# Causal corners of the expert batches added by VectorE, fewer four-byte softmax chunks, and a new order table

## The chip, the cores and the metric

One NeuronCore of a Trainium2 chip runs the whole program. The metric is the device time of one execution in microseconds (us), and lower is better. The kernel before takes 612.18 us (median of three runs, 612.18 to 612.55).

## What is computed

A first attention has 8 heads in each of 4 batches over 768 positions, each query sees only the keys of its own hash bucket. Its output, 512 wide, feeds four causal attention "experts" per batch, which a top-2 gate mixes.

```python
mask = q_bucket[:, :, :, None] == k_bucket[:, :, None, :]
scores = np.where(mask, scale * np.matmul(q, k.transpose(0, 1, 3, 2)), -1e9)
attn = softmax(scores)
x = np.matmul(attn, v)            # (B, S, 512) once the heads stand side by side
logits = x @ w_gate               # the two best experts of each row, softmax weights w
for e in range(E):                # E = 4
    q, k, v = x @ wq[e], x @ wk[e], x @ wv[e]
    scores = np.where(causal, -1e9, scale * (q @ k.transpose(0, 2, 1)))
    ye = softmax(scores) @ v @ wo[e]
    out += (w of expert e, 0 where it isn't among the two) * ye
```

## The kernel before

The work is cut into units: 32 heads `("L", b, h)` and 16 experts `("M", b, e)`, which the list `seq` puts in a row: the eight heads of batch 0, then the heads of each later batch with the experts of the batch before it between them, and the experts of batch 3 at the end. A unit's place in the list is `pos`, from 0.

Each unit is an attention over 768 by 768 scores. `max_steps` forms the scores once on TensorE into the two PSUM buffers `mx`, and VectorE takes row maxima from them into `pm` (`pmw` for the first heads). `shift_steps` turns the maxima into a row of the query operand. `s_unit` forms the scores a second time, in chunks of up to 512 columns in the three PSUM buffers `st`, nine chunks for a head and six for an expert. For a chunk ScalarE takes two exponentials, `p` in four bytes and `ph` in two; GpSimd subtracts them into the remainder `pl`; and TensorE multiplies, for each block of 128 columns, `ph` by the upper half of v (`vh`, `mvh` for experts), `ph` by its lower half (`vl`, `mvl`) and `pl` by the upper half, all into the PSUM tile `o`, which `normalise` empties on VectorE into `xp` (heads) or `yn` (experts).

Two choices in `s_unit` concern us.

- Chunk 4 (`WHOLE`) of a head with `pos` under `NWHOLE` is kept whole: one exponential into a four-byte tile `pf`, no remainder, and per block one four-byte matmul by `vf`. With `NWHOLE = 12` these are the eight heads of batch 0 and the first four of batch 1.
- An expert's blocks on the diagonal need the causal corner. In batches that aren't in `MASKV`, TensorE adds it with one more 128x128 matmul of `mask_t` by the identity into the chunk, ahead of the chunk's second matmul. In batches in `MASKV`, here batch 3 alone, VectorE adds `mask_t` to the finished block in PSUM, and the chunk's exponentials wait for that.

`vproj_steps` makes v of the experts and the gate's logits, for each of six row tiles of a batch: TensorE into a PSUM buffer `misc`, ScalarE copies the upper half (`mvh`), VectorE forms the lower half (`mvl`), and ScalarE or VectorE copies four columns of logits (`lg`).

Around these run loads, halves and copies of operands between partitions (DMAs `qk<-qk`, `qk<-M`, all issued by SP's queue), transposes and projections. None of it is issued as written: a `Recorder` notes each operation, and `schedule` (all instructions are issued at line 183) puts them in the order of the table `ORDER`. For each step the table names the next operation, which engine takes it where there is a choice (`copy` may go to ScalarE or VectorE, some remainders to VectorE or GpSimd), and how many filler matmuls on the tile `busy` stand ahead of it. Each engine then works through its own part strictly in order. Line numbers of the profile are therefore all L183, and tile names tell the operations apart.

Of the kernel before, what the change touches and what calls it, by code (L numbers as in the profile page):

```python
# [211 lines left out]
MASKV = (3,)  # L212

ORDER = (
    "c-rlJX^bT2d0u^A-S^#9)z#Hqec#9QOwUZubkEGr%+9gPy}3M>BE4K*wnBljgy^6sSdb`LzLX$jC_r)|IdG6fN}@!8%mju5<X;5A2y6sF{v<G9|L_k(K%D%E6XpG?yLV=m%ZL=0<nFQ`"
    "u#fGj<E!_3-sgSZueymOS(bR7m!mVhfcQ902b^h9dwZSBE#Ig1smPWxIaNhLj1aY)&SbQXmN7F{W;O1!IP^u`u!}Y)m|K{toz_{l#fXTe1eYDMh{{)sMT(+UR#w&vYlV2Jc~J~<nS7<v"
    "Zu^B&{qLs2YPHsE)~k&|g$m-JU>6JdEFg#?KNAJbl2TeMd4+U3c<wp<#TRqUW;5Gpq&jSy)=TNaL(e@&IaS-f%9qsW+?A({OOFaya}PcG*rV3tfxef?2*QI8p2<G+P&(^l-@o|r!2jIm"
    "KIdy1<J+Eh{kr!FPgM<b>$e{N&EIVPhIy(pSm_|=@0sSH($EE5$*Da6vvVO5+5~j#IHJ~y)Y#liZ_LmfkEPKlyDLeh)fpm5l9sC8s{ib>jsEGUpZ28$obQX;!vrb7m8jDZJEG_*^+yyX"
    "tDGiKb|1Y3j%B%5r+DTTus3cv&h_i^=x||Om6bDRw3U^sM^GLVYa7Z^->m`EgR58Dt+6^9jrw-kto1t!J+r;64zx<S{Ip)x^+I8Jd08yWDonkiC~&cv9K2RDo)`5M1%e_9sl{`4A6c&X"
    "?;o*zfMd5gcLv#U3IIW~I5V0+&4}yk%Gz2wofZRARijAO6*aBKvIjHnjYc^^lDu#n1Ops8X^!)6i&CkSO2eT|&&fy;Yd>TA`tiS;+#(5S>U?Sf%L_wK3{$Bfv^1mtx^0@?1RDHRpA6R!"  # L220
    "4gDompWp@6!>+3KXRsMXYsx7@7HkLzBulT?*N?$<1zEBHl9}N5{!n&o!zh>Ka<eHn8k#07Y~?pMWicy5B(I5U!cfV%g#we$v+ZRDFXeKqTaTjZG*VIhw%}{usNLihS|JGY;ZppC#l=NK"
    "GoJq<lM37IOh{+bY1j2>2z0uY_8L(Tc<{EAo&iEwk^>{3&;MyEK6B=bcL>o4yvAZ<#agI)DW#H1nGh8Vn_24!xd|-QHDt@3hMQb}#VB_qLoXE@jfPb~mi4_>>whFEQqdanbo8ZKwpeVp"
    "yPaOIT!y!p@T1U}q3~l|Di%r!HcKb)ukyvXP+lmP%a0WPftD)>bvHgd%w{9ESj@PP<+)8MbU-vlqbQdP!U$w4=!lbR^(&QTbLju_gO$qVXP&8Cx?F}qV_bwo;+t%BN8~(KF##bB3!gdI"
    "29dznq<VTMn>#ob39==_bMbKuhx+PqWHTB1nw-w%C@G7@6ql~eu*Gd{!SToApN$i^?)n72KOFilWW!R<bG<+NGa^1-y3^_8^9wLp^?IsSLp3)jp8`-@1gX{H_yic$S{laZY#S0d<)_xx"
    "b}sMiEcRgsv^B$x8#mgoz8WiEF`FIJw!YY)zVHRjKJz(wd;3iDuyJuq*G(e<qhpQ09$<Cx+_@njfNOKTdUG*>Y)~z}LqN6Ls;a5=L4q4M1_QOUSTpLCFB+Yb5Ze<}I;~386YIiKP_0H~"
    "-U+F^4f9a3fi6YIyBV-b#w#PADWuXTB7XL)dnQ4ySq|JFlXp4CfjGg`x&9tH?Z%5I-~f5MIpla=t8xCkWz~Y<@Q^uh%yl#CSPsGBl5OoStgfEAIgO9Zu)2ETLU85EmGr_T!14o@buIzR"
    "S`Lz!)+x0^pE|X5@fcKPcjJKx)G@uaHQL)l5KI&fmsbxDS4SfO1aW(9irrmjxV{e4GrD~FvUAB>USD0il>7xD$aWJZbYo+Gd3kel8IcgPOPibQieW4n!vqKuMbKfh<tONC`<E^~x_|ND"
    "mmUKAi-#V%aPh(Y!*iFkCv^QkK*~;LRZ>-pQ0dI6GYXv7+Eq4;@pyYY-b=8xWtztLacXl4<AoJnKfitpHZ~6QeZyFP7J_x^`bdFGIDJ|hq3szKB*Hlr4)DMOr<GxEskjWI{m0we@O-nh"
    "DGLujy!NzmH9t^Fmr56{3m2NjbLWZ=Xv>o+F1+$efqD7mLZ|TA&#Ir%{<cv1^c26JAgkEacL{i^Fpj^i2EO}Efd9rDzW@5`-fOQdn0l(sjeh&L1)M5dFO^Dektm$wP?V9Vw&(FFN7pS&"
    "*CD8eE<c8AH9=AGc`i?ss^5>ROt(_0NY$!VrZOc4J~Z+N2M0j8e6!hV4mXEu!^a<gytzuQDBo!COAi9#D+x9)Z{m%OCpONVdyHEcJu+IjcI|6lLl3_C>Vy0H`w`pWb}q5{lD_!>rJo*;"  # L230
    "7e)zy374O}JOL!a=6K^#boMy@))CZ))_?ix)#snDoPGA$e*&lshZj$u-aGxB@6a^=yT40+`-N|Pi+ldlBrGqy@u|O0K)?R_a|bVNJWqY%8{hpdZ1@)7muUR)uVZ@ajW?LDzYd^Zd+oJf"
    "r<cz@y}bS~x5n?W+*iNKaliK}$8lR6H{N-X<39iS&r|p_470g8{u-dcz542_+*eq3_$77%*x>VzKF+etRdAlXFvT<64Tcd#K3XgZLKuE`gJt2bPx1URT>I{2o?luXz3{>dX6k{#*|R*~"
    "gTNnLU!$JlfXLUh#<VzHDRRG>)z};h>YF<}JnSBHx_dv{>hA9Dw!2ggxE%3g{usd3C@KM8t?pE-RRw0)j7xu7jC(^Q%c`tqR_gVPoG6GSud6*dSm8XeTJ2YVSnavlrE*yU(UK&ji-Jn3"
    "_lnNCOL02!4vxd~5E~AEEM*bCSzbCuw2OdYZq4;v$<hl9V=(bXVd^HrVi-zLo&gf586#l<Qj-{)KbeKfIsw5n1;fxZI$PvP+WwnK_GXz-lF|}U3d$P{{$Xk)ic8`IZBe`Qjjq@eMMaUM"
    "f|$eEEplM?<(FTEm}K~6{shRl1dVSz#Y^IEJpuUjDj)O0LO2;uCgTf^AUHf+aF(}Cr(?Q?X|P<i$1qT~iRP*FAG}G+H$e;kOq?N=qBZs}InKNZng(|KcZU5sE8YrL_>@3CWu*rs5jJIb"
    "{jtY(S&n;%Wf%7r$JSfHiCmTDnslS_e3(`OhWQiXz;QPL?o|DVwvPKOy4E692VxkVK87mHpNF-<U^EKD(VB*bpm@1#5YXwNF=}+DGTs>8g2O5BV!N%ovW$rwV!DG{VzXA)mY1to;2?6C"
    "1NxD=SOsQ-b2<GSj3r02n`k30fjd5u+|2p&S&$_TCFw+K48vfWHs~@>FBgkEm(QnCosP_L#9xVyoy(PTeBy?hCm<%yE0?P|6#7iP&Zdd|VG@gg=#9T2ElnoFt%qh;HkRc_JiQSvJRODx"
    "S1#+erAeA?+XnbT4HMcctn9E-rDCP(DcO{a5^HR3X2tPXgCg+en;;@vL1tqkpsBPkLFhK58M^gvsamTA@01B-U~W2{Oa4eX;AX`&X3G5$w5dF#>nEg!Qg5~dS&)9I)@WohkpMZqD~j8M"
    "B^P2>6c+=L;y9hN);WgV)LGrs8bfxKWmO)6%!^{7#<IdOWQ7BEAJWy}bRAMwkrjEOSdzpaF|Y;?o<|IO0u1v*h36U40SP>pVwjB$hSQkcT{te#6e49aCu!NVEFf?s<`_u*TfKhZcYzJ3"
    "7&hWVi4!fB<wAm)EeWC2XTmm=2%YU~3kwS-V!l~@<Bd1y)!vVOq?ZR|X8+|9z&>e$WRN(T7W@5Tvs#D3z|%}2U&$j<#7^2Yy40d3JfZ2j>*gwzFq>r@<_Nvsk9(rqVOoN!O<epodD?)M"  # L240
    "+NcPm%@E;4eZdpT9nfYeo0Z_b6$FIk$j{~ePY%j%c--sL6Aw<idd6`gHxoR)9_n^rr<zS{(XL$q$H>#*^Bj)$wNN2F8+38td;UvmTUl}y)`ae~fAOMh9LF}R>+vLwbv+vcC&M57;0I$o"
    "QrFjmtuVc@to|cabs=0mb%tXdUP(patLZHHl)?~m*LS5gN&3{MEI~xNAS^En9hhh7c1VR`CZ)QrO7Z{t(^gmM*p|$1@O2&v4s_b8b{w7t+_r7iBV9Km!$l~pE|{t$E{KArkxE5Ra|G0y"
    "rZYsHY3?LgUSxUB;cXjZc60OKz}RQ>(;SU?U>(%an+$9~gEs-j0wd%94Z2K=bY_d*B*!hj4K7?Dm6oGv-3FSd+rR{`&VXXNRijc_s!07Kln3R?zb)Gf3si3b>R6R#p&lf{TP}+frhw|*"
    "xX^CI<+xsd>fn|v__g{%BFGGcs!GzkungVY$D1^hr#&xMDxs)Q$YwAM0|f90`Fsy*tsp{W$|#1Qi=b3cH4zXDE;f%9qBP+oS|OK)Y9m3WtB}T(|3(G~8J={fa$f6bxYatyP9PAS8%1J9"
    "g`@f7a5R#<f@hkNtNu|6l8dyCUB+^xf^CcO%1Ukp>D(e=0T=@n<b;x>&!n&@s%=eFRj9toGk@hPK>|_sQ-y-(iNzF=>O5pi_Clhp5sW9D9&c@>>A-Q^sahRhg3vpYmsZ44YMzn;3d+)%"
    "tt~OTx3_)zG~OLY+rp_+g0Q(M814|m`~uUG+D?>-1JlEIB}kNFk}jG3eL<l2)c``0VUr~*XJtZXL(+R47MeJgXhci+F?)>bLL!iSI35gy)S^!@B)|+Fv23l@t8q}FnJIe}u`cGrn>$*T"
    "3y0qFJTLjDM@zJ#(LAUgVvnC7H+|(q@qgVEWGD?-fXRlbwM0l0dN6>h!y{>Jja}d{P=jN!@HQa2mq(<XL>w1IE{5}!4LNljOH;5e7J3eFmw`(!mo0d=!W5ZNt%e!C`YoZ?%T^#iYHhyS"
    "mgAdcw$wNdrcP7{)u?J|(v4%FGV%J|Zj{S;%>kirJ|D*Ib}^09<#M$eR4SPaaQFNSzjFS(3!516^1;DhEN`WP3GF?bw&+yy)-*Lu=hc>~W*5t9y0<|W3NN+W+^!a{@=!Y(2y9os&*I*M"
    "d_g@h(@~izdtPC)GQr*+!|av}Birw5T8<$JVDpes)~|tf_?Bb2nd$OLcZvg@=UaTUiT+rw*A=;{C&!UxGBf7J2Aw@zSdh#N%RUAK(X>8AqD$7qS~3_UzLDk9VtQr*A^%o5S4eC<HBCTX"
    "Q(3+At6EWw6Q#?rlWn2Q>-x?0f?8x`2#q;TbyfAt)Uv{|Wm$%)07dGQRT(I+DATSF(iddb&sw(Z$;kF>+X8X0H1o3rut`#vsx=spIeC}{EzZ_7l}D5t37;>UmmJ5ie`edBk-Bn_Qd01t"  # L250
    "W~quH$vs)S9nw_cKTREv1eREXJ{0O&Adkn^>C?ZWs%NnzOPd;eCd#6D4Nkly(hxSSg8O}%Ya~XxK|OdgJI;ax*&G|OnQohHwancyH6`63T&mZ#T5WNuR(m`N(az3}-qaET($i(3-E&)P"
# [1214 lines left out]
```

## Time and profile before

| | us |
|---|---|
| median of 3 runs | 612.18 |
| the profiled execution | 612.32 |
| its span, first to last instruction | 610.5 |
| TensorE busy | 591.4 (97%) |
| VectorE busy | 524.0 (86%) |
| ScalarE busy | 516.8 (85%) |
| GpSimd busy | 471.5 (77%) |

The granted TensorE clock is full throughout. Busy time of TensorE is no measure of its rate, because matmuls overlap: a 128x512 matmul in two bytes is shown 0.38 us long, while the next one starts 0.22 us after it. What a matmul costs is read from the distance between starts. 1.8 us of the execution lie outside the span.

### The profile page before, as it was taken

The page shows a single profiled execution, that of the slowest core. Times are in us where ns is not written, and L with a number is a line of the kernel's source. Part 1 is how long each engine was busy: PE and PEld are TensorE (multiplying, and loading weights), DVE is VectorE, ACT ScalarE, POOL GpSimd, SP SyncE. Part 2 cuts the span into 40 slices and gives each one's busy share as a digit, 9 for nine tenths or more (in the row PEclk, how much of TensorE's full clock was granted, in tenths as well). Part 3 has the DMA queues.
Part 4 walks back from the last instruction along what each step waited for, and adds up shares of the span by engine and source line. Part 5 has one row for each costly group of instructions (what it writes and reads, how often), then busy time and mean ns, then how long its engine had stood idle before and what let it go on. Part 6 is the DMA issues. An engine that isn't in the chain of part 4 may idle for free.

```text
span 610.5 us, 20339 instructions
## 1 busy us (share of the span) xinstructions
PE 591.4 (97%) x7754; PEld 432.8 (71%) x7754; DVE 524.0 (86%) x1440; ACT 516.8 (85%) x1132; POOL 471.5 (77%) x540
## 2 busy tenths in 40 slices
...
GB/s 188 169 189 195 81 146 68 56 99 48 153 40 58 41 87 61 102 104 32 92 89 87 37 119 101 58 83 73 68 87 75 45 48 42 16 21 28 87 79 104
DMA packets 36313, 51.22 MB, mean 84 GB/s; under 512 B 8212, under 2 KB 26104, under 8 KB 36216
## 3 DMA queue, kind: packets, MB, share of 16 engines
...
q8 instruction: 61, 1.00, 0.7%
q14 instruction: 36, 0.29, 0.2%
q10 hardware_dynamic: 160, 0.00, 0.0%
...
## 4 chain that ended last, share of the span: by engine, by line
PE 67%; DVE 17%; ACT 8%; issue 3%; POOL 2%; DMA 2%; SPq 1%; DVEq 0%; ACTq 0%; POOLq 0%
PE misc L183 22%; PE st L183 19%; PE o L183 16%; PE mx L183 10%; DVE pm L183 6%; ACT p L183 3%; ACT ph L183 3%; DVE qk L183 2%; DVE xt L183 1%; DVE misc L183 1%; POOL pl L183 1%; DVE pmw L183 1%; DMA natq<-in_q_dram 1%; SPq L183 1%; ACT xt L183 1%
## 5 line engine op out<-in xcount | busy, mean ns | idle before, releaser
L183 POOL TENSOR_TENSOR pl<-p,ph 128x512 f16<-128x512 f32 x370 | 409.4, 1126 | 111.3 <-ACT p L183 32.4
L183 PE MATMUL st<-qk 128*128 128x512 f16 (+12 forms) x928 | 229.7, 325 | 2.1 <-ACT p L183 1.0
L183 ACT ACTIVATE ph<-st 128x512 f16<-128x512 f32 x372 | 214.0, 609 | 15.2 <-PE st L183 11.1
L183 ACT ACTIVATE p<-st 128x512 f32<-128x512 f32 x372 | 215.9, 609 | 11.7 <-PE st L183 8.9
L183 PEld LDWEIGHTS <-ph 128*128 128x128 f16 x2880 | 168.1, 98 | 35.5 <-issue 6.5
L183 DVE TENSOR_REDUCE pm<-mx 128x2 f32<-128x512 f32 (+1 forms) x248 | 162.9, 673 | 11.2 <-PE mx L183 8.3
L183 PEld LDWEIGHTS <-pl 128*128 128x128 f16 x1440 | 133.3, 97 | 16.8 <-issue 4.1
L183 PEld LDWEIGHTS <-qk 128*128 128x128 f16 (+4 forms) x1248 | 109.1, 98 | 46.9 <-issue 9.2
L183 PE MATMUL mx<-qk 76*128 76x512 f16 (+2 forms) x464 | 134.3, 326 | 7.2 <-DVE qk L183 4.5
L183 PE MATMUL o<-vh,ph 128*128 128x65 f16 (+1 forms) x1104 | 138.8, 194 | 0.3 <-DVE xp L183 0.3
L183 PE MATMUL o<-vh,pl 128*128 128x65 f16 (+1 forms) x1104 | 138.8, 193 | 0.3 <-POOL pl L183 0.3
L183 PE MATMUL o<-vl,ph 128*128 128x64 f16 x1104 | 138.1, 192 | 0.0
L183 PE MATMUL misc<-xt,wqk_h 128*128 128x384 f16 x256 | 58.6, 325 | 0.0
L183 DVE CUSTOM_DVE_ANT_0 scrap<-mx,causal 128x512 bf16<-128x512 f32 (+2 forms) x96 | 44.4, 462 | 8.8 <-PE mx L183 7.0
L183 DVE TENSOR_REDUCE pmw<-mx 128x2 f32<-128x512 f32 x68 | 44.9, 681 | 2.3 <-PE mx L183 2.0
L183 PE MATMUL o<-mvh,pl 128*128 128x65 f16 x336 | 40.6, 193 | 0.6 <-DVE yn L183 0.6
L183 PE MATMUL o<-mvl,ph 128*128 128x64 f16 x336 | 40.9, 192 | 0.0
L183 PE MATMUL o<-mvh,ph 128*128 128x65 f16 x336 | 40.6, 193 | 0.1
L183 POOL TENSOR_TENSOR vl<-vf,vh 128x384 f16<-128x384 f32 x32 | 29.5, 928 | 11.1 <-PE misc L183 5.1
L183 PEld LDWEIGHTS <-xt 128*128 128x128 f16 x324 | 29.6, 97 | 10.7 <-issue 1.8
L183 PEld LDWEIGHTS <-wqk_h 128*128 128x128 f16 x256 | 24.0, 97 | 14.5 <-issue 1.6
L183 PE MATMUL misc<-wvg_h,xt 128*128 128x260 f16 x192 | 32.1, 274 | 0.7 <-ACT row L183 0.7
...
## 6 DMA issues: line engine op xcount, KB each, us to landing
qk<-qk SPq DMA_DIRECT2D x128, 96.0 KB
...
```

What stands on the lines that cost most here:

```text
L183: getattr(getattr(self.nc, e), m)(*[real(x) for x in args], **{k: real(x) for k, x in kw.items()})
```

## The change

- `NWHOLE` goes from 12 to 4: heads 4 to 7 of batch 0 and 0 to 3 of batch 1 do chunk 4 as any other chunk.
- `MASKV` takes in all four batches: VectorE adds the corners of all 16 experts.
- In `vproj_steps` the copy of the logits stands ahead of the lower half of v.
- `ORDER` is another table.

```diff
-NWHOLE = 12
+NWHOLE = 4
...
-MASKV = (3,)
+MASKV = (0, 1, 2, 3)

 ORDER = (
-    "c-rlJX^bT2d0u^A-S^#9)z#Hqec#9QOwUZubkEGr%+9gPy}3M>BE4K*wnBljgy^6sSdb`LzLX$jC_r)|IdG6fN}@!8%mju5<X;5A2y6sF{v<G9|L_k(K%D%E6XpG?yLV=m%ZL=0<nFQ`"
...
+    "c-rlpd5oO*dEe)~@B5nfo%_CzotfR)oxOLt7s<Uy?k-PB6c3%GDO;{6Tc#2_k?J#Q1*1_?*+!k(Nfkgz8^=x10tK1|ZBn3rr74`I{ii_xNCUJ$il!}s_W8Xtvj<I@qO_DqYCga_GrRL%"
...
             nc.scalar.activation(MVH[:, i, :, 0:D], pv, AF.Copy, scale=2.0 ** -16)
+            nc.copy(lg[:, i], p[:, E * D:W], XS[b][:, 2:3])
             nc.vector.scalar_tensor_tensor(MVL[:, i], pv, 2.0 ** -16, MVH[:, i, :, 0:D], op0=OP.mult, op1=OP.subtract)
-            nc.copy(lg[:, i], p[:, E * D:W], XS[b][:, 2:3])
             yield 864
```

What the program holds afterwards: on TensorE 72 corner matmuls fewer, 32 four-byte matmuls fewer (two records each) and 32 x 3 two-byte ones more, and 63 fillers where there were 75. On ScalarE eight exponentials more. On GpSimd eight remainders of 128x512 more. On VectorE 72 corner additions more. Copies with a choice move on balance from ScalarE to VectorE: `lg` 6, `row` 4, `fr` 4, `ot` 2, `vs` 2, `vcol` 2, `yth` 1 and one copy of the last output; the other way go `qk` 2 and `xt` 1. SP's queue has the same transfers in another order.

The first place is the third expert of batch 0. On TensorE, before, a corner (`st<-mask_t,ident`) stands between the two matmuls of a chunk:

```order
L183 LDWEIGHTS pl
L183 MATMUL o<-vh_465,pl 128x65
L183 LDWEIGHTS qk
L183 MATMUL st<-qk 128x512
L183 LDWEIGHTS ident_78
L183 MATMUL st<-mask_t,ident_78 128x128
L183 LDWEIGHTS qk
L183 MATMUL st<-qk 128x512
```

In the change no row of TensorE names `mask_t`, and VectorE has, for the same expert:

```order
L183 TENSOR_REDUCE pm_257<-mx 128x2 x2
L183 TENSOR_SCALAR misc<-cs_476 128x1
L183 TENSOR_SCALAR rden<-o,cs_1494 128x6
L183 RECIPROCAL cs_476<-misc 128x1
L183 RECIPROCAL rden<-rden 128x6
L183 TENSOR_TENSOR st<-st,mask_t 128x128
L183 TENSOR_TENSOR xp<-o,rden 128x6x64
L183 TENSOR_TENSOR st<-st,mask_t 128x128
L183 TENSOR_REDUCE pm_257<-mx 128x2 x2
```

The corner additions have moved in among the row maxima (`pm<-mx`) and the emptying of `o` (`xp`), which TensorE also waits for.

The second place is chunk 4 of head 4 of batch 0 on ScalarE, before:

```order
L183 ACTIVATE p_1672<-st 128x512
L183 ACTIVATE vh_465<-vf_376 128x6x64
L183 ACTIVATE pf<-st 128x512
L183 ACTIVATE p_1735<-st 128x512
L183 ACTIVATE ph<-st 128x512 x2
L183 ACTIVATE xt<-misc,xs 128x3x128
```

and in the change:

```order
L183 ACTIVATE vh_166<-vf_106 128x6x64
L183 ACTIVATE ph<-st 128x512 x2
L183 ACTIVATE p_1738<-st 128x512
L183 ACTIVATE p_1759<-st 128x512
L183 ACTIVATE p_1764<-st 128x512
L183 ACTIVATE ph<-st 128x512 x2
```

The single `pf` has become a `p` and a `ph`, and a copy of the transposed heads (`xt<-misc`) has left this place.

The third place is the start of SP's queue, which issues all loads, before:

```order
L183 DMA natq<-in_q_dram 128x384
L183 DMA natk<-in_k_dram 128x384
L183 DMA natq<-in_q_dram 128x384
L183 DMA natk<-in_k_dram 128x384
L183 DMA natq<-in_q_dram 128x768
L183 DMA natk<-in_k_dram 128x768
L183 DMA natv<-in_v_dram 128x768 x2
```

and in the change:

```order
L183 DMA natq<-in_q_dram 128x384
L183 DMA natk<-in_k_dram 128x384 x2
L183 DMA natq<-in_q_dram 128x384
L183 DMA wst<-in_moe_wq_dram 128x1024
L183 DMA natq<-in_q_dram 128x768
L183 DMA natk<-in_k_dram 128x768
L183 DMA natv<-in_v_dram 128x768
```

A load of an expert weight (`wst`, 512 KB) has moved ahead of the loads of the second pair of heads (the two of 128x768); before, it stood at the queue's 28th row.

## Rows read from the trace of the kernel before

**Rows 1.** The page's first part: busy time and share of each engine.

```profile
PE 591.4 (97%) x7754; PEld 432.8 (71%) x7754; DVE 524.0 (86%) x1440; ACT 516.8 (85%) x1132; POOL 471.5 (77%) x540
```

**Rows 2.** Busy time by stretch: length, PE, PEld, DVE, ACT, POOL, PEclk, DMA, GB/s.

```profile
0.00:73.00 73.00, 69.73 (x817) 54.22 (x818) 65.83 (x151) 64.62 (x130) 68.72 (x151) 1.00 0.61 172
73.00:122.00 49.00, 48.49 (x661) 38.70 (x660) 45.10 (x107) 48.47 (x102) 45.91 (x44) 1.00 0.33 84
122.00:178.00 56.00, 54.64 (x696) 41.45 (x695) 49.75 (x145) 49.97 (x120) 39.95 (x40) 1.00 0.34 93
...
220.00:553.00 333.00, 325.62 (x4426) 233.51 (x4423) 283.71 (x789) 278.34 (x616) 255.04 (x246) 1.00 0.25 68
```

**Rows 3.** What TensorE waited for: us in total, times, longest us.

```profile
PE mx L183 <- DVE qk L183: 4.5, 10, 0.9
...
PE mx L183 <- DVE pm L183: 2.3, 5, 0.8
...
PE st L183 <- DVE st L183: 0.5, 1, 0.5
```

**Rows 4.** Timeline, one such wait: start us, length us, engine, operation, idle before.

```profile
399.77 0.55 DVE L183 TENSOR_TENSOR qk<-mx,qk 128x384 f16<-128x384 f32 x1
...
400.36 0.38 PE L183 MATMUL mx<-qk 65*128 65x256 f16 x2 [0.60 <-DVE qk L183]
```

**Rows 5.** Timeline of TensorE around a corner of an expert of batch 0.

```profile
174.83 0.22 PE L183 MATMUL st<-mask_t,ident 128*128 128x128 bf16 x1
174.89 0.19 PE L183 MATMUL o<-vl,ph 128*128 128x64 f16 x1
```

**Rows 6.** Timeline of TensorE around two four-byte chunks (x4: two blocks).

```profile
102.46 0.19 PE L183 MATMUL o<-vh,pl 128*128 128x66 f16 x1
...
102.55 0.19 PE L183 MATMUL o<-vh,pl 128*128 128x66 f16 x1
...
102.95 0.64 PE L183 MATMUL o<-vf,pf 128*128 128x66 f32 x4
103.42 0.17 PE L183 MATMUL misc<-ones,vl 128*128 128x1 f16 x1
...
126.15 0.56 PE L183 MATMUL o<-vf,pf 128*128 128x66 f32 x4
126.55 0.38 PE L183 MATMUL mx<-qk 76*128 76x256 f16 x2
```

**Rows 7.** Groups of instructions by shape: count | busy us, mean ns | idle before.

```profile
L183 POOL TENSOR_TENSOR pl<-p,ph 128x512 f16<-128x512 f32 x339 | 385.7, 1157 | 102.8 <-ACT p L183 29.0 <-ACT ph L183 21.9 <-PE misc L183 20.9
...
L183 ACT ACTIVATE ph<-st 128x512 f16<-128x512 f32 x340 | 201.1, 625 | 12.4 <-PE st L183 10.7 <-PE o L183 0.8 <-DVE st L183 0.2
...
L183 DVE TENSOR_TENSOR st<-st,mask_t 128x128 f32<-128x128 f32 x24 | 6.8, 293 | 3.3 <-PE st L183 2.6 <-ACT ph L183 0.2
...
L183 DVE TENSOR_SCALAR ot<-misc,xs 128x512 f32<-128x512 f32 x7 | 5.2, 749 | 2.1 <-PE misc L183 2.0 <-PE o L183 0.2
...
L183 DVE CAST row<-misc 12x128 f16<-12x128 f32 x11 | 3.0, 275 | 2.6 <-PE misc L183 1.8 <-ACT fr L183 0.7
...
L183 DVE TENSOR_SCALAR lg<-misc,xs 128x4 f32<-128x4 f32 x11 | 2.3, 219 | 1.4 <-PE misc L183 0.9 <-ACT mvh L183 0.5
```

**Rows 8.** Instructions on the tile mask_t: who waited for them (us, times).

```profile
  ACT ph L183: 2.7, 3
  ACT p L183: 1.0, 3
  PE st L183: 0.5, 1
```

**Rows 9.** The chain of waits at the start, and DMA rate in 40 slices of 0:30.

```profile
2.92 5.70 DMA natq<-in_q_dram
...
16.80 1.21 PE st L183 x4
...
GB/s 0 0 72 299 307 256 168 231 240 287 360 414 336 134 49 94 242 240 88 0 61 178 148 21 68 160 162 156 315 191 83 135 246 307 33 74 258 332 237 215
```

More of the change, by code (lines that the diff above doesn't have):

```diff
@@ new lines @@
+    "xFDY2#X5IRJexXm=FD^Z5T5l39aYrTlZvhy+VZd}p0Of3avh(k)i!Gz(t2}zbyb*DM0t9;)3GNeCTw+av0QG+^Bv%2*oMclSw&IGBd1O^#S`*obM$;h899hF+#3obMN1{JSPZ61;dmw)"
+    "32w9Ld?=T5GOlUsg6DZ@gdl_x2qPYk8%8v07(qQ*7XCV+CA3&Jo6X4@r|>#I8=O&cQZ}6F(}3;o#LwG-WS@eZcin{Pa?ZaAZDq{#o$z8w+qGjo!gfTq!r`#x#^cWSoZ$E@xYVcv-)y_l"
+    "1Gtfh97Y7=F=yfctmCLAWei)<V6f9MLk`0jnqeCMQ5zE00K<^|+tY!tuE#<lT2+D-4=iaZO2;s4I<FTqOG|&u#;2#_iNwUjlq3maAv`xV^+elACbuUt$)OY5+uLa;l@fQyn=F+|&TLL("
+    "-V@T{u}NX#$tOFbsZ{D+*i!Gjlj;*f7FN@Vgl~bk|GUqo_P7ymG_KXEiRQ8T(WAAM^~%bsKP8E|M1qECiA~3hwKZ+x;t2OtBzgzTqbR!QT$e0tw42GmR0KWqpN1T#?KrX8JMU;GPc|A2"
@@ new lines @@
+    "&wIV-c?L;l%d4y9>~f;0miowlCaY>DGcuexNVx}9I!G#2=u!?{rjprg@=5TRL@HE`r_-gspGc-Fl}b9ju#oE=pE!7UQp~36^<ptxsYHt~jsn;;EmIB^rrZ!kEiIirYo4hxhFL1v)0@|>"
+    "74L-U<|i%d#EJ9cKh26w87(TET+r*($`Eh_sJlDr_Qb^8KB|yYVr*p!v2_qDU1~P}b!nqoRebVFJ)IstDa_8wO<A7&Uvj-JFOA6&iAu@aaMPh|bw5YFm6iGQ`O3L-9`Ev+mrdmM(v|H5"
+    "HI3SsYv`u+zB$z8heJO=Z?k>cZJN>!dOSGV9-3BIsxRuF{jC0yowt3GStD&(x@nr4L5=FFskT~6EtEw{?r5?7^X<0k4g<7*0XeT}s-~(sRZr(zf0AxC*+wJVy_sUYUeDF`;H&j~B~z)C"
+    "!{K;3A9u==lkIXDow<`8>yyk-u|mNHUu)ziB5;OitX8u}N2`g1U0e@^gJRrW0Yb~m%WlN-f*yG5H1At~%JCK!Cd8aA#?G9HdEGd3+#5G;IKgPcfdr840SAY}>B+EV&(5YsJ8-DpwW>KW"
```

132 lines of the change are left out of this document (63 added, 69 removed).

## The prediction

> **What bounds the kernel now.** I began with the busy times of the engines. TensorE is busy 97% of the span, VectorE 86%, ScalarE 85%, GpSimd 77% [rows 1]. Busy time of TensorE overstates it, so I asked next, stretch by stretch, whether another engine is nearer its end. In most of the program it isn't: from 220 to 553 us TensorE is busy 325.62 of 333 us, VectorE 283.71, ScalarE 278.34, GpSimd 255.04. The heads of batch 0 are different. In the first 73 us GpSimd works 68.72, and from 73 to 122 us, where heads 4 to 7 run, ScalarE works 48.47 of 49 us and GpSimd 45.91 [rows 2]. There all four engines are near their limit, and work taken off TensorE alone need not shorten anything.
>
> Then I read what TensorE waits for. Its dearest named wait once the program runs is for VectorE to give back an `mx` buffer: 4.5 us in 10 waits behind operand halves (`qk`) and 2.3 us in 5 behind row maxima (`pm`), 6.8 us together [rows 3]. One of them in detail: VectorE ends `qk<-mx,qk` at 400.32, and the next score matmul into `mx` starts at 400.36 after 0.60 us of idling [rows 4]. So TensorE's stream sets the time, with small waits for VectorE on top. The change takes work off the first and puts it on the second.
>
> **The change part by part.** The sum is made against the profiled execution, 612.32 us, of which 1.8 us lie outside its span; it is 0.14 us above the median of the runs.
>
> *Corners off TensorE.* 72 matmuls of 128x128 go. One starts at 174.83 and the next matmul at 174.89 [rows 5], 0.06 us by start; rounding leaves 0.05 to 0.07. 72 x 0.06 = **-4.3 us** (3.6 to 5.0), on the path, because TensorE streams without a break there. The Trainium skill's page "TensorE: Matmul & The Clock Gate", section "Back-to-back issue gap", gives about 81 ns for a matmul of 128 columns in a stream of weight loads and matmuls; by it the term would be an estimate of -5.8 us. The trace shows 0.06 us in such a stream, and the row decides.
>
> *Four-byte chunks back to two bytes.* Eight heads, four blocks each. Three two-byte matmuls of a block take 0.09 us (102.46 to 102.55). Two four-byte blocks take 0.47 us (102.95 to 103.42) at one place and 0.40 us (126.15 to 126.55) at another [rows 6]. A pair of blocks therefore saves 0.47 - 0.18 = 0.29 or 0.40 - 0.18 = 0.22 us, and 16 pairs save 4.6 or 3.5 us. I take **-4.0 us**, between the two.
>
> *Fillers.* Twelve fewer, at 0.06 us like any matmul of 128 columns. They stand at the start, where TensorE joins the chain of waits only at 16.80 us [rows 9], so they count nothing; if they did, it would be -0.7.
>
> TensorE's stream thus loses 8.3 us. Now what the other engines get.
>
> *ScalarE and GpSimd.* Eight exponentials at 0.625 us make 5.0 us on ScalarE, eight remainders at 1.157 us make 9.3 us on GpSimd [rows 7]. ScalarE hands over about as much in copies (below), so its total stays near 517 us. GpSimd rises to about 481 us, 79% of a 607 us run. Half of the heads concerned lie between 73 and 122 us. There 4 x 1.157 = 4.6 us would bring GpSimd from 45.91 to 50.5 us in a stretch of 49. It fits only if remainders or other subtractions move out of the stretch; the other half, 122 to 178 us, has 16 us of GpSimd idle [rows 2]. I count this at nothing in the sum and keep its price for a rival.
>
> *VectorE.* 72 corner additions at 0.293 us are 21.1 us [rows 7]. The copies it takes over are 6 x 0.219 (`lg`), 4 x 0.275 (`row`), 4 `fr` of the same shape as `row` and taken at its price, and 2 x 0.749 (`ot`): 1.3 + 1.1 + 1.1 + 1.5 = 5.0 us; the rest that comes and goes I take as cancelling. VectorE goes from 524.0 to about 550 us, 91% of 607. Two waits can come of it.
>
> First, the chunk is held between its matmul and its exponentials. Behind a corner addition the queue is in order, so ScalarE's next exponentials stand still, and after them the `st` buffer that TensorE wants. In batch 3, where VectorE does this already, 24 additions cost TensorE 0.5 us once, and ScalarE 2.7 + 1.0 = 3.7 us [rows 8]. Three times as many additions give 1.5 us of TensorE's waits; nothing at the one end, and at the other all of ScalarE's waits handed on, 3 x 3.7 = 11.1 us. I take **+1.5 us**, what TensorE itself showed.
>
> Second, row maxima stand behind the additions in VectorE's queue, as the second piece of order in the section on the change shows, and `mx` comes free later. If every one of the 15 waits now had an addition of 0.293 us ahead of it, that is 4.4 us more. The new table could also cure them all, -6.8 us. I take a third of the first, **+1.5 us**, because VectorE has less idle time to hide in, 60 us instead of 88.
>
> *Logits ahead of the lower half.* Both read the same PSUM buffer, and it comes free after the later of them either way: nothing. What hides it is that TensorE has a second `misc` buffer; if that cover failed the price would be one `lg`, 0.219 us, in each of 24 row tiles, 5 us at most [rows 7].
>
> *The transfers.* SP issues as many as before. At the start, though, a 512 KB weight load now stands ahead of the second pair's query load, and that load lies on the chain of waits for 5.70 us. At some 300 GB/s, as DMA ran in the fourth and fifth slices, 524 kB take 1.75 us [rows 9]. ScalarE's own order before that load is also longer by three copies, so part is covered: between 0 and 1.8, I take **+0.5 us**.
>
> Sum: 612.3 - 4.3 - 4.0 + 1.5 + 1.5 + 0.5 = 607.5 on the profiled execution, **607.4 us** at the level of the median. The table as a whole was made anew, and beyond these places I cannot price it; it may add or cure a wait anywhere, which widens the range and not the sum.
>
> **The rivals.**
>
> *The stream is paid in full.* The new order finds room for the additions, and no new wait appears: 612.2 - 8.3 = 603.9 us. For it speaks that VectorE has 14% of idle time and that TensorE's waits in batch 3 were short. Against it, that an order can do nothing where four engines are near full. If the new table also cures some 2.5 of the 6.8 us at `mx`, it comes to 601.5.
>
> *The early heads don't pay.* From 73 to 122 us GpSimd would need 50.5 us, while TensorE's saving there, half of 4.0, would ask for 47. If GpSimd wins, 3.5 us of the forecast are lost: 610.9 us. The 45.91 and 48.47 of 49 us speak for it. Against it speaks that the second piece of order shows a copy leaving ScalarE at just this place, so the load there isn't what it was.
>
> *VectorE becomes the bound in the expert stretches.* The additions' waits on ScalarE pass to TensorE through the three `st` buffers: 11.1 us instead of 1.5, at the same other terms 607.4 + 9.6 = 617.0 us, and 615.0 if the rest costs nothing. It decides against the change as soon as an addition costs TensorE on average (8.3 + 1.2) / 72 = 0.13 us, less than half its own length. For it: 91% load on an engine with a strict order. Against it: 0.5 us for 24 in batch 3 [rows 8], though the last experts run where VectorE is far less loaded.
>
> *The four-byte blocks are cheap.* If one cost four passes of a two-byte matmul, 4 x 0.03 = 0.12 us, the chunks would save 32 x (0.12 - 0.09) = 1.0 us instead of 4.0, and the run take 610.4 us. The 0.40 and 0.47 us for two blocks [rows 6] are well above 0.24, so this has little left. It is what the Trainium skill's page "FP8 and Floating Point Precision", section "TensorE Precision Notes", would lead one to: it counts four passes for a true FP32 product.
>
> **How the numbers follow.** The forecast gets 0.42, full payment 0.22, the early heads 0.20, VectorE as the bound 0.14, cheap four-byte blocks 0.02. A measurement of this kernel tells 0.2% (1.2 us) from no change, so faster means under 610.96 and slower over 613.40. Forecast and full payment lie under it; the early heads' 610.9 lies at the line and is split, and the cheap blocks go to faster: 0.42 + 0.22 + 0.08 + 0.02, say 0.74 faster. 0.12 fall within 0.2% and 0.14 are slower. For the range I go down to the full payment with waits at `mx` cured, 601.5, and up to 613.5, the early heads' 610.9 with 2.6 us more at `mx`, short of the 4.4 that bounds it. That leaves out most of the VectorE case above and little below, about 0.2 in all.
>
> **What would show it.** Right: no corner matmul on TensorE and 96 corner additions on VectorE at about 0.29 us; VectorE's busy time near 550 us; a third of the four-byte matmuls `o<-vf,pf` (16 instructions where there were 48); waits of TensorE for `st` behind VectorE of 1 to 3 us in all, and waits at `mx` of 7 to 10. The stretch of heads 4 to 7 would be shorter by 1 to 2 us, and the start would not be late by more than 1 us at the first exponential. Wrong: a first exponential well after 18 us; GpSimd without a gap through heads 4 to 7 and that stretch as long as before; or waits of TensorE for VectorE that sum to more than 16 us, which would mean that the additions set the time.

## The result and the profile after

The changed kernel takes **620.59 us** (median of four runs, 619.45 to 623.62) against 612.18 (612.17 to 612.55): ratio 1.0143, 95% interval 1.0113 to 1.0174. It is slower by 8.4 us, and lies above the range that was given. The profiled execution is one of 619.45 us with a span of 617.7.

The page's first part of the changed kernel, in the form of [rows 1]:

```profile
PE 588.1 (95%) x7702; PEld 423.2 (69%) x7702; DVE 538.4 (87%) x1531; ACT 517.6 (84%) x1121; POOL 479.8 (78%) x548
```

TensorE does less, VectorE is busy 14 us more, and every share has hardly moved. Busy time by stretch, columns as in [rows 2] (length, PE, PEld, DVE, ACT, POOL, granted clock, DMA share, GB/s):

```profile
0.00:73.00 73.00, 70.03 (x817) 54.83 (x818) 67.46 (x154) 66.58 (x136) 70.27 (x150) 1.00 0.63 175
73.00:122.00 49.00, 47.88 (x690) 36.55 (x690) 46.71 (x112) 47.84 (x100) 47.47 (x45) 1.00 0.36 93
122.00:178.00 56.00, 53.96 (x723) 39.20 (x720) 50.84 (x155) 50.97 (x117) 45.11 (x48) 1.00 0.24 63
...
220.00:553.00 333.00, 321.55 (x4318) 227.42 (x4316) 289.85 (x837) 278.86 (x608) 252.99 (x244) 0.99 0.25 67
...
443.00:447.00 4.00, 4.00 (x31) 2.38 (x29) 1.76 (x5) 1.68 (x4) 1.19 (x2) 0.57 0.17 38
...
443.00:444.00 1.00, 1.00 (x4) 0.30 (x2) 0.49 (x2) 0.91 (x2) 0.04 (x1) 0.50 0.02 5
```

In the long stretch TensorE does fewer matmuls in the same time, and the clock, 1.00 throughout before, is 0.99 there. The last two rows show where: for some four microseconds from 443 us TensorE runs mostly at the lower of its two levels, 0.50 or 1.2 of 2.4 GHz. In the kernel before, the same stretch is at full clock:

```profile
443.00:447.00 4.00, 4.00 (x58) 2.55 (x55) 2.52 (x5) 2.60 (x8) 1.55 (x2) 1.00 0.31 98
```

What TensorE waited for (us in total, times, longest), against [rows 3]:

```profile
PE mx L183 <- DVE qk L183: 5.6, 6, 1.8
PE mx L183 <- DVE pm L183: 3.3, 5, 1.4
...
PE misc L183 <- DVE xt L183: 2.4, 2, 1.4
PE o L183 <- DVE xp L183: 1.9, 4, 1.1
PE o L183 <- DVE yn L183: 1.1, 2, 0.6
PE misc L183 <- DVE qk L183: 1.0, 1, 1.0
...
PE st L183 <- DVE st L183: 0.8, 1, 0.8
```

All rows of this view that name VectorE sum to 19.3 us, where they summed to 8.2 before. The waits at `mx` are fewer and longer (1.8 us where the longest was 0.9), and there are new ones for `xt`, `xp` and `qk`. The corner additions, against [rows 8]:

```profile
L183 DVE TENSOR_TENSOR st<-st,mask_t x96: 273/290/300, 173.8 to 603.9; 128x128 f32<-128x128 f32 x96
...
  ACT ph L183: 6.0, 7
  ACT p L183: 4.3, 10
  PE st L183: 0.8, 1
```

ScalarE waits 10.3 us for them and TensorE 0.8.

Where along the program is the time lost? The instruction by which VectorE empties `o` ends a unit. Here are the 12th, the 32nd, the 40th and the 48th (the first half of its queries), of before and then of the changed kernel (start, length):

```profile
183.52 0.56 DVE L183 TENSOR_TENSOR xp<-o,rden 128x384 f32<-128x384 f32 x1
...
421.50 0.56 DVE L183 TENSOR_TENSOR xp<-o,rden 128x384 f32<-128x384 f32 x1
...
515.25 0.56 DVE L183 TENSOR_TENSOR yn<-o,rden 128x384 f32<-128x384 f32 x1
...
598.71 0.36 DVE L183 TENSOR_TENSOR yn<-o,rden 128x192 f32<-128x192 f32 x1
```

```profile
181.82 0.55 DVE L183 TENSOR_TENSOR xp<-o,rden 128x384 f32<-128x384 f32 x1
...
421.43 0.55 DVE L183 TENSOR_TENSOR xp<-o,rden 128x384 f32<-128x384 f32 x1
...
519.07 0.55 DVE L183 TENSOR_TENSOR yn<-o,rden 128x384 f32<-128x384 f32 x1
...
605.99 0.36 DVE L183 TENSOR_TENSOR yn<-o,rden 128x192 f32<-128x192 f32 x1
```

The changed kernel is 1.7 us ahead after the twelfth unit, level after the 32nd, and 7.3 behind after the 48th. It loses in the second half, where no chunk is done differently and only the corners and the order differ.

One number is worked out from the traces: **TensorE's stream**, the sum over its matmuls of the distance to the next start, each taken at most at the lower quartile of its shape (columns and type). It is 549.6 us before and 540.3 after, an estimate that moves by some 0.4 us with the way the quartile is taken. The work came off TensorE as forecast, about 9.3 us. All else in the span grew from 60.9 to 77.4, by 16.5 us, and 10.5 of these are idle time of TensorE, 29.6 us (617.7 - 588.1) where it was 19.1 (610.5 - 591.4).

### The profile page after: what moved, and what is told of

Its sections match the earlier page's. It is cut to its first block, busy times and chain, and to the rows that moved or that the text cites. A ratio compares the mean times of both kernels' runs of the same rounds, so it can differ in the third digit from the quotient of the medians.

```text
span 617.7 us, 20417 instructions
## 1 busy us (share of the span) xinstructions
PE 588.1 (95%) x7702; PEld 423.2 (69%) x7702; DVE 538.4 (87%) x1531; ACT 517.6 (84%) x1121; POOL 479.8 (78%) x548
## 4 chain that ended last, share of the span: by engine, by line
PE 69%; DVE 15%; ACT 10%; issue 3%; POOL 1%; DMA 1%; DVEq 0%; ACTq 0%; POOLq 0%
PE misc L183 22%; PE st L183 20%; PE o L183 16%; PE mx L183 11%; DVE pm L183 4%; ACT p L183 4%; ACT ph L183 3%; DVE qk L183 2%; DVE scrap L183 2%; DVE xt L183 1%; DVE misc L183 1%; DVE st L183 1%; ACT mx L183 1%; DMA qk<-qk 1%; POOL pl L183 1%
## 5 line engine op out<-in xcount | busy, mean ns | idle before, releaser
L183 POOL TENSOR_TENSOR pl<-p,ph 128x512 f16<-128x512 f32 (+1 forms) x378 | 418.0, 1127 | 117.3 <-ACT p L183 42.1
L183 ACT ACTIVATE p<-st 128x512 f32<-128x512 f32 (+1 forms) x380 | 219.3, 608 | 18.5 <-PE st L183 5.1
L183 ACT ACTIVATE ph<-st 128x512 f16<-128x512 f32 (+1 forms) x380 | 218.7, 607 | 19.0 <-PE st L183 12.1
L183 PE MATMUL st<-qk 128*128 128x256 f16 (+12 forms) x928 | 227.4, 326 | 2.6 <-DVE st L183 0.8
L183 PEld LDWEIGHTS <-pl 128*128 128x128 f16 x1472 | 136.2, 97 | 13.6 <-issue 1.9
L183 PE MATMUL mx<-qk 76*128 76x512 f16 (+2 forms) x464 | 131.5, 326 | 10.2 <-DVE qk L183 5.6
L183 PE MATMUL o<-vh,ph 128*128 128x66 f16 (+1 forms) x1136 | 140.2, 194 | 0.6 <-DVE yn L183 0.6
L183 PE MATMUL o<-vh,pl 128*128 128x66 f16 (+1 forms) x1136 | 139.1, 193 | 0.0
L183 PEld LDWEIGHTS <-xt 128*128 128x128 f16 x324 | 29.6, 97 | 11.1 <-issue 2.0
L183 DVE TENSOR_TENSOR st<-st,mask_t 128x128 f32<-128x128 f32 x96 | 27.6, 292 | 6.3 <-PE st L183 5.0
```

Source lines behind the costliest of these rows:

```text
L183: getattr(getattr(self.nc, e), m)(*[real(x) for x in args], **{k: real(x) for k, x in kw.items()})
```

## The experiments

The change has three parts that can be separated: who adds the corners, how many chunk-4s are whole, and the order. For each kernel below the order of one of the two was kept as it stands and only the operations of the named part were exchanged: a corner matmul stands right behind the first matmul of its chunk, a corner addition right behind the chunk's last matmul, and the steps of a chunk-4 where the other form of it stood. "Old order" is that of the kernel before. "New order" is the rest of the change as a whole: the sequence of the steps, the engine that takes each copy, the fillers, and the place of the logits. The theories at the start were three: the additions cost the time (1), the order does (2), or the chunks do (3).

**Corners back on TensorE, new order.** Against the changed kernel:

```diff
-MASKV = (0, 1, 2, 3)
+MASKV = (3,)
```

> The changed kernel with its own order; only the 72 corners of batches 0 to 2 go back to TensorE, each right behind the first matmul of its chunk (four chunk-4s stay whole). Theory 1 (the 72 additions on VectorE hold up what TensorE waits for: mx, o and misc buffers): the additions' stalls go and 4.3 us of matmuls come back, so 608 to 613 us. Theory 2 (the new order itself loses the time, whoever adds the corners): 4.3 us more on a stream that waits as before, 621 to 625 us. Theory 3 (the eight chunks done in two bytes cost more than they save): 618 to 623 us, for the additions would be nearly free.

Measured: 619.15 us, ratio to before 1.0104 (1.0088 to 1.0121). Theory 1 is out: without these additions the kernel comes nowhere near 613 us. The time lies in the range of theory 3; theory 2 expected a little more, since it charged the 4.3 us of matmuls that went back to TensorE, and they cost nothing.

**Chunk-4s whole again, new order** (`NWHOLE = 12`; in this order `vf` is refilled sooner, so the four-byte blocks of heads 4 and 5 multiply a later pair's v):

> The changed kernel with its own order; only the eight chunk-4s of heads 4 to 11 are whole again (one exponential, one four-byte matmul per block). Theory 1 (additions): about 4.0 us of matmuls come back and the additions stay, 622 to 626 us. Theory 2 (order): the same 622 to 626 us. Theory 3 (chunks): 612 to 616 us.

Measured: 620.82 us, 1.0131 (1.0114 to 1.0148). Theory 3 is out for this order. Four microseconds of TensorE's work came back, and again the time did not move, just under the 622 us from which theories 1 and 2 expected it. The twelfth unit ended 1.2 us later than in the changed kernel (182.99 against 181.82, by the starts as above).

**Corners to VectorE, old order** (`MASKV = (0, 1, 2, 3)` in the kernel before):

> The kernel before with its own order; only the 72 corners go from TensorE to VectorE, each addition behind the last matmul of its chunk. Theory 1 (additions): 616 to 624 us. Theory 2 (order): 607 to 610 us, the 4.3 us of matmuls less some 1.5 of waits. Theory 3 (chunks): 607 to 610 us too.

Measured: 630.82 us, 1.0299 (1.0282 to 1.0316), above even theory 1's range. In the old order the additions are very dear. TensorE's waits there:

```profile
PE mx L183 <- DVE pm L183: 8.5, 20, 1.2
...
PE st L183 <- ACT p L183: 2.2, 6, 0.6
PE st L183 <- ACT ph L183: 2.2, 5, 0.8
PE misc L183 <- DVE negh L183: 2.0, 4, 0.9
```

Both waits that the prediction named are there: `mx` behind row maxima, 2.3 us in 5 before and now 8.5 in 20, and `st` behind the held exponentials, 1.0 + 0.5 us before and now 2.2 + 2.2.

**Chunk-4s in two bytes, old order** (`NWHOLE = 4` in the kernel before):

> The kernel before with its own order and its corners on TensorE; only the eight chunk-4s of heads 4 to 11 are done in two bytes. Theories 1 and 2: 608 to 611 us, 4.0 us of matmuls less what GpSimd and ScalarE cannot take in heads 4 to 7. Theory 3 (chunks): 614 to 620 us.

Measured: 618.19 us, 1.0095 (1.0078 to 1.0112), in theory 3's range: in the old order the chunks do cost. Most of the loss, 4.6 us, has arisen by the end of the twelfth unit, and the trace names GpSimd:

```profile
PE o L183 <- POOL pl L183: 3.2, 6, 1.2
```

This row was 0.3 us in one wait before. Five of the six waits, 3.0 us, lie between 80 and 150 us, where the heads concerned run. The remainders that I had costed at nothing hold up the products by `pl`.

**Both parts undone, new order** (`MASKV = (3,)`, `NWHOLE = 12` in the changed kernel), and **both parts, old order**:

> The new order with both parts undone: corners of batches 0 to 2 on TensorE again, the eight chunk-4s whole again. In some heads the four-byte blocks multiply a later pair's v, since this order refills that tile sooner. What differs from the kernel before is the order alone. Theory 2 (the order loses the time): 617 to 621 us. Theory 1 (additions lose it): 610 to 613 us.

> The order of before with both parts: corners by VectorE and the eight chunk-4s in two bytes. If the two costs measured alone, 18.4 and 5.8 us, add up: 636 to 638 us. If they share waits: 630 to 635 us.

Measured: 622.30 us, 1.0163 (1.0146 to 1.0181), and 636.10 us, 1.0388 (1.0370 to 1.0405). In the old order the two costs add up. The new order costs 9.6 us with the very work of the kernel before, a little more than theory 2's range. Here are the ends of the 24th and the 48th unit with this work, of before and then in the new order:

```profile
329.46 0.55 DVE L183 TENSOR_TENSOR xp<-o,rden 128x384 f32<-128x384 f32 x1
...
598.71 0.36 DVE L183 TENSOR_TENSOR yn<-o,rden 128x192 f32<-128x192 f32 x1
```

```profile
329.17 0.56 DVE L183 TENSOR_TENSOR xp<-o,rden 128x384 f32<-128x384 f32 x1
...
608.80 0.36 DVE L183 TENSOR_TENSOR yn<-o,rden 128x192 f32<-128x192 f32 x1
```

Up to the 24th unit the two orders are level; the 10 us arise behind it.

| | corners TensorE, 12 whole | corners VectorE, 12 whole | corners TensorE, 4 whole | corners VectorE, 4 whole |
|---|---|---|---|---|
| old order | 612.2 to 612.7 | 630.8 | 618.2 | 636.1 |
| new order | 622.3 | 620.8 | 619.2 | 620.6 |

The old order punishes both departures from its own parts; the new one takes all four sets within some 3 us and is slower than the kernel before with each.

**Corners left out**, once in the old order and once in the new:

```diff
-                    elif diag:
-                        nc.tensor.matmul(p[:, o:o + 128], ident16, mask_t, start=False, stop=False)
```

> The kernel before; the 72 corners of batches 0 to 2 are left out altogether, on every engine. Theory A (TensorE's stream sets the time, 0.06 us each come off): 607 to 609 us. Theory B (the engines are so near each other that TensorE's gaps take it back): 610 to 613 us.

> The changed kernel; the 72 additions of batches 0 to 2 are left out altogether, on every engine. Theory 1 (additions lose the time): 607 to 612 us. Theory 2 (the order loses it, the additions cost little in it): 614 to 619 us.

Measured: 612.21 us, 0.9994 (0.9984 to 1.0003), and 618.82 us, 1.0090 (1.0069 to 1.0112), as theory B and theory 2 expected. The first is the finding of this study. 72 matmuls less on TensorE, its stream shorter by 4.0 us (549.6 to 545.6; most corners of before start 0.055 to 0.058 us ahead of the next matmul), and the time is what it was. The trace shows where part of it went: the distances ahead of matmuls into `mx`, over the quartiles of the stream, sum to 13.8 us before and 16.0 here. So TensorE comes to the same buffers earlier and gets them no sooner. The units end where they ended (12th, 32nd, 40th, 48th):

```profile
183.51 0.56 DVE L183 TENSOR_TENSOR xp<-o,rden 128x384 f32<-128x384 f32 x1
...
421.89 0.56 DVE L183 TENSOR_TENSOR xp<-o,rden 128x384 f32<-128x384 f32 x1
...
514.93 0.56 DVE L183 TENSOR_TENSOR yn<-o,rden 128x384 f32<-128x384 f32 x1
...
598.66 0.36 DVE L183 TENSOR_TENSOR yn<-o,rden 128x192 f32<-128x192 f32 x1
```

Measured from this kernel, an addition on VectorE costs (630.82 - 612.21) / 72 = 0.26 us in the old order, nearly its whole length, and in the new one (620.59 - 618.82) / 72 = 0.02, or 0.05 by the ratios to before (1.0143 and 1.0090); either is within the scatter of these two kernels' runs (616.57 to 620.17 and 619.45 to 623.62). So the new order does hide most of the additions' length; what it loses, it loses for the larger part without them, 6.1 us of 8.4. Its longest waits are the same in the kernel without the additions:

```profile
PE mx L183 <- DVE qk L183: 5.7, 6, 1.8
PE mx L183 <- DVE pm L183: 3.1, 5, 1.4
...
PE misc L183 <- DVE xt L183: 2.4, 2, 1.4
```

**Additions that nobody waits for.** In the old order, with the corners on TensorE, VectorE gets 72 more instructions at the places of its additions:

```diff
+                for j, q0, q1 in chunks[c]:
+                    if not lsh and q0 == j * 128 and u[1] not in MASKV:
+                        nc.vector.tensor_tensor(spare, ident, ident, op=OP.add)
```

> The kernel before, corners on TensorE; VectorE gets 72 additions of 128x128 in four bytes between SBUF tiles, at the places where its corner additions stood, and nobody uses their result. Theory A (VectorE's own queue is full there: any instruction of 0.2 to 0.3 us costs its length): 624 to 631 us. Theory B (the cost is that the exponentials wait for the corner): 612 to 615 us.

Measured: 646.41 us, 1.0569 (1.0523 to 1.0615). This is more than either theory, since these instructions took up to 1.27 us instead of 0.2 to 0.3 (see the last section). VectorE's busy time rose by 38.9 us (524.0 to 562.9) and the kernel's by 33.7, 0.87 us per us; the real additions raised it by 16.8 over the kernel without corners (524.2 to 541.0) and the time by 18.6. A part of the 33.7 goes with a lower clock, 0.984 to 0.993 in these four runs. No exponential waits for these additions, so time in VectorE's own queue costs by itself: the row maxima come later, and the wait at `mx` behind `pm`, 13.1 us in 22 times, is the largest of all. How much of the 18.6 us the held exponentials add is not separated.

```profile
PE mx L183 <- DVE pm L183: 13.1, 22, 1.8
```

**The copies as before, new order.** Each copy that may go to ScalarE or VectorE goes where the kernel before has it, 119 of them in both directions; only the table's row of choices differs.

> The changed kernel and its order; each copy that ScalarE or VectorE may take is put on the engine that it has in the kernel before, 119 of them in both directions, so that VectorE has 17 fewer. Theory 2a (the new order loses time because VectorE took on copies): 613 to 617 us. Theory 2b (it is the order of the steps, whoever copies; or the copies' new places fit the new order): 620 to 627 us.

Measured: 646.43 us, 1.0547 (1.0531 to 1.0563), far above both ranges. VectorE's load is lower, 535.6 us with 19 instructions fewer, and the kernel 26 us slower. Nothing speaks for theory 2a: where each copy goes belongs to the order, and taken alone the old choice does harm. For the same reason this run can't price the copies by themselves.

**Joining the orders.** Corners on TensorE, four whole chunk-4s, the new order up to the end of a unit and the old one from there on:

> Corners on TensorE in batches 0 to 2, chunk-4s of heads 4 to 11 in two bytes; the new order up to the end of the 12th unit, the old order from there on. The 12th unit ended at 182.7 us in the new order with this work and at 184.1 us before. If the stretches keep their pace: 610.5 to 611.5 us. If the joint costs what the head gains: 612 to 614 us.

> The same work as in the last one, with the joint at the end of the 24th unit, 329.6 us in the new order with this work and 330.0 before. Theory 2 (what the new order loses, it loses in its second half): 611 to 613 us, where the new order throughout took 619.2. If the loss lies in the first half or in the work itself: 616 to 620 us.

Measured: 611.63 us, 0.9985 (0.9976 to 0.9994), and 612.09 us, 0.9989 (0.9980 to 0.9998). The first lies between its two ranges, the second in theory 2's. The same work in the new order throughout took 619.2. So the loss lies in the new order behind the 24th unit, as the unit ends say. The beginning gains about a microsecond with the chunks in two bytes; with the old work it gains nothing (the last instruction of the twelfth unit starts at 183.68 us in the new order and at 183.52 before). In both joined kernels the logits stand behind the lower half of v, as before.

**Is VectorE the bound, then?** If 17 us more on VectorE cost 18.6, less should give time back. In both orders the row maxima of heads in batches 1 to 3 were shortened:

```diff
+                if u[1]:
+                    src = src[:, :, 0:192]
```

> The kernel before with its own order; each row-maximum reduction of a head in batches 1 to 3 reads 192 of each 256 columns, so the maxima leave out a quarter of the keys: 216 instructions on VectorE, each shorter by some 0.13 us, 28 us less in all, and nothing else is changed. Theory A (VectorE's queue sets the time in the expert stretches): 587 to 597 us. Theory B (VectorE is only one of several engines at the limit; added work hurts, removed work gives little): 604 to 612 us.

> The changed kernel with its own order; the same 216 reductions are shortened in the same way. Theory A' (the new order's waits hang on VectorE as well): 596 to 606 us. Theory B' (they hang on how the steps follow each other): 614 to 620 us.

> The kernel before with the same shortened reductions, and with the 72 corners of batches 0 to 2 left out on every engine. If TensorE sets the time once VectorE is relieved: 3 to 4.5 us less than with the shortened reductions alone. If not: within 1 us of it.

Measured: 609.89 us, 0.9953 (0.9936 to 0.9970); 615.62 us, 1.0047 (1.0033 to 1.0062); 608.48 us, 0.9931 (0.9915 to 0.9948). The instructions did become shorter (count, busy us, mean ns; before, then in the first of these kernels):

```profile
L183 DVE TENSOR_REDUCE pm<-mx 128x2 f32<-128x512 f32 x216 | 143.2, 681 | 9.6 <-PE mx L183 7.1 <-PE o L183 1.4
```

```profile
L183 DVE TENSOR_REDUCE pm<-mx 128x2 f32<-128x384 f32 x216 | 116.9, 552 | 18.5 <-PE mx L183 13.7 <-PE o L183 1.5
```

26 us less in these rows, 20.8 in VectorE's busy time, and 2.8 us of the kernel's. What VectorE saved it spent idle: 104.4 us (607.6 - 503.2) where it was 86.5 (610.5 - 524.0), and half of that increase stands before these same instructions, 18.5 us where it was 9.6, waiting for TensorE. So VectorE is not the bound in the sense that its load sets the time; theories B and B' hold. Nor does TensorE become the bound once VectorE is relieved: its 72 corners then give 1.4 us, between the two expectations. In the new order the relief gives 5.0 us, part of which is the clock (0.993 to 0.999 in these runs, 0.991 to 0.997 in those of the changed kernel).

The Trainium skill's page "Perfetto Trace Analysis", section "Identifying the Most-Contended Engine", advises to find the engine with the highest occupancy and to work on that first; for TensorE it warns that the busy share of matmuls is no good measure, and takes the share of weight loads and the share of the peak arithmetic instead. By weight loads TensorE stands at 71% [rows 1], so VectorE, at 86%, would come first. The runs don't bear it out: 20.8 us off VectorE gave 2.8. Nor would the busiest engine by matmuls have been a better choice: 4.0 us off TensorE (97%) gave 0.5.

**Filling the waits.** If an engine in strict order waits although later work in its row could run, moving that work ahead must give time back. In the changed kernel 255, and in the spliced one 182, of TensorE's matmuls of probabilities by v were moved ahead of matmuls that waited in the trace; nothing else changed.

> The changed kernel; 255 of TensorE's matmuls of probabilities by v are moved ahead of 18 matmuls that waited there for VectorE, ScalarE or a transfer, by as many as fit the wait (8 us of work at 0.03 us each); their order among themselves, every other engine's order and all the work stay. Theory R (the row's order wastes the time): 612 to 616 us. Theory P (waits are passed on: what runs early is missing as cover later): 618 to 622 us.

> The kernel with the joint at the end of the 12th unit, with 182 such matmuls moved ahead of 14 waiting ones in the same manner (5.6 us of work). Theory R: 606 to 609 us. Theory P: 610 to 613 us.

Measured: 616.06 us, 1.0067 (1.0050 to 1.0084), and 610.92 us, 0.9977 (0.9967 to 0.9986). The first lies just above theory R's range and gives back 4.5 of the 8.4 us; the second lies in theory P's. Here is the stretch of the lower clock again, in the first kernel:

```profile
443.00:447.00 4.00, 4.00 (x55) 2.45 (x54) 3.33 (x9) 3.54 (x8) 1.88 (x2) 1.00 0.39 115
```

55 matmuls at full clock where the changed kernel did 31 at 0.57. In its four runs the clock is 0.997 to 1.000. The profiled execution of the second kernel was 2.1 us ahead of before at the end of the 32nd unit and lost over one of them behind 434 us. There the move had filled a first wait for VectorE, but the next one, which had lost its cover to it, took 1.31 us, and the clock fell:

```profile
436.00:440.00 4.00, 3.88 (x41) 3.16 (x42) 3.23 (x8) 2.17 (x5) 1.59 (x3) 0.60 0.02 4
```

This execution is the slowest of ten, 611.55 us at a mean clock of 0.995; the other nine ran at 0.999 or more. With the moves at 435 and 487 us left out (the two waits then take 0.48 and 0.92 us, and the second ends at 436.11 us where it ended at 436.12, so the first had only been passed on):

> The spliced kernel with 142 of the 182 matmuls moved: the moves ahead of the waits at 435 and 487 us are left out. Theory R (a filled wait is gained where the next one keeps its cover): 608.5 to 610 us. Theory P (passed on): 610.5 to 612 us, as before these moves.

Measured: **610.66 us**, 0.9968 (0.9956 to 0.9980), at the lower end of theory P's range. So in this kernel filled waits were for the most part passed on. It is 2.0 us faster than the kernel before as run beside it (612.65) and 9.9 faster than the changed one, the lowest median of all kernels here that leave no work out; the kernel with all the moves, 0.9977 (0.9967 to 0.9986), isn't told from it.

## Why the prediction was wrong

**What failed first is the sentence "So TensorE's stream sets the time, with small waits for VectorE on top".** The stream's terms were sized well: the corners forecast at -4.3 measure 4.0 us of stream, the chunks at -4.0 measure 4.2 (549.6 to 545.4 in the old order), both as estimates from the stream. But the time didn't follow the stream. The corners off TensorE gave 0.5 us (by the interval, 1.0 faster to 0.2 slower), and the chunks cost 5.8 in the old order. I had seen that four engines are near their limit from 73 to 122 us and thought it special to that stretch; from 220 to 553 us I took TensorE's 325.62 of 333 us [rows 2] as the mark of a bound. That row couldn't show it: without 4 us of work TensorE was as busy as before, 97%.

**What failed most is the sentence "beyond these places I cannot price it; it may add or cure a wait anywhere, which widens the range and not the sum".** The order alone costs 9.6 us with the old work (622.3 against 612.7). This is larger than any term of the sum, and it was put at nothing because no row of before speaks of it. The range took in no more than a few microseconds for it.

The rival that VectorE becomes the bound, 617.0 us, comes nearest to the measured time, but by luck: it charges the additions, and the runs charge the order.

Point by point:

- *Corners, -4.3.* Off TensorE as forecast; worth nothing by itself in either order.
- *Chunks, -4.0.* Worth 1.2 us at the twelfth unit in the new order and nothing at the end. The rival of the early heads was right on its place: heads 4 to 7 took 48.0 us (72.0 to 120.0) where they took 47.8 (73.6 to 121.4), so the mark of a stretch shorter by 1 to 2 us was missed. GpSimd works 47.47 of 49 us there, against 45.91 [rows 2]; the 4.6 us of remainders were made room for in part. The words "I count this at nothing" failed in the old order, where they cost 3.2 us of waits for `pl` (0.3 before).
- *Additions: waits at `st`, +1.5.* 0.8 us in the changed kernel, ScalarE's share 10.3 against the 11.1 taken as the upper end. The size was fair, for this order. VectorE's busy time came to 538.4 us and not near 550: the additions raised it by 11.0 us in this order (from 527.4 without them) and by 16.8 in the old one, not by the 21.1 that their number times their length gives. In the old order an addition costs 0.26 us, twice the 0.13 from which the rival decides; that rival, 617.0 us, describes the kernel that has the additions without a new order (630.8), and there it was too small.
- *Waits at `mx`, +1.5.* 8.9 us against 6.8, so +2.1. The size came out by luck, since the cause isn't the additions: the waits stand in the kernel without them too (8.8). The mark "waits for VectorE over 16 us would mean that the additions set the time" was met, 19.3, and misled: without the 72 additions the sum is 18.5.
- *Head load, +0.5.* Wrong: the first exponential starts at 17.07 us instead of 17.62, and the fourth unit ends 1.5 us earlier.
- *Logits ahead, nothing.* Not tried alone. TensorE's waits name no `lg`. ScalarE's do: it waits for `lg` before `mvh` for 9.6 us in 6 times, where it was 1.5 in 2, but before other instructions of this step it waits less. No run undoes this in the second half, so it stays a part of what is called the order here.

**How the loss comes about.** Look at one place, the longest wait of the changed kernel, in its timeline of VectorE and of TensorE (start, length, and the idle time before in brackets):

```profile
438.48 0.69 DVE L183 TENSOR_REDUCE pm<-mx 128x1 f32<-128x512 f32 x1 [0.47 <-PE mx L183]
439.20 0.28 DVE L183 TENSOR_SCALAR fr<-misc 12x128 f16<-12x128 f32 x1
439.51 0.42 DVE L183 CAST yth<-misc 128x256 f16<-128x256 f32 x1
439.97 0.42 DVE L183 TENSOR_TENSOR ytl<-misc,yth 128x256 f16<-128x256 f32 x1
440.31 0.55 DVE L183 CAST qk<-mx 128x384 f16<-128x384 f32 x1
440.90 0.56 DVE L183 TENSOR_TENSOR qk<-mx,qk 128x384 f16<-128x384 f32 x1
```

```profile
438.06 0.38 PE L183 MATMUL mx<-qk 65*128 65x512 f16 x1 [0.83 <-DVE qk L183]
...
441.51 0.27 PE L183 MATMUL mx<-qk 65*128 65x256 f16 x1 [1.77 <-DVE qk L183]
```

VectorE first waits for TensorE (0.47), then TensorE for the last of six instructions of VectorE; no corner addition is among them. Each engine's row is strict, each waits for the other in turn, and at this place neither is the bound by itself. That work taken from one engine turns into its waiting fits two experiments (the corners left out, the maxima shortened), and that work put on VectorE costs nearly its length fits two others in the old order; that knots like this one are the reason throughout is argued from this place and not shown. After the two waits TensorE runs at the lower clock from 443 us on, 31 matmuls in four microseconds where the kernel before has 58.

How the 8.4 us split is shown only in part: 4.5 come back when the waits are filled and the clock stays up. Some of it is the clock alone: the four runs of the changed kernel lie 4.2 us apart with their mean clocks 0.006 apart, 0.7 us per thousandth, and those of the kernel with whole chunks 3.6 us over 0.008, 0.45 per thousandth. From this an estimate of the changed kernel at full clock is 617.4 to 618.1 us (from 619.45 at 0.997), still 5 to 6 us slower than before. The other 3.9 us arise late: the kernel with filled waits ends the 36th unit 1.3 us ahead of before and the 48th 3.4 behind. What they hang on, and why the new order for the second half has longer waits than the old one, stays open.
